# Keys and queries loaded in pieces twice as large in an attention and feed-forward kernel: 24 key loads of 768 KB in place of 48 of 384 KB, and the adds that pool them spread evenly

## The chip, the cores and the metric

One Trainium2 chip, one of its cores. The metric is the device time of one execution in microseconds (us). Three runs of the kernel before took 1876.52, 1888.96 and 1879.23 us; their median is 1879.23.

## The reference

Four batches of 12288 queries attend to 768 pooled keys, which are also the values; the result goes through a feed-forward block with a gated softmax and a layer norm. All in float32, with the feed-forward weights as float64:

```
kv_pool = kv.reshape(B, H//4, 4, W//4, 4, C).mean(axis=(2, 4))     # B=4, H=384, W=32, C=128
k = v = kv_pool.reshape(B, -1, C) @ w_sr                           # 768 keys
s = (q @ k.transpose(0, 2, 1)) / sqrt(C)                           # 12288 x 768 per batch
a = exp(s - max);  a /= a.sum + 1e-9;  x = a @ v
h = x @ w_in                                                       # 128 -> 1024
solu = h * softmax(h)
out = layernorm(solu) * g_ln @ w_out                               # 1024 -> 128
```

## The kernel before

**Tiles and slots.** The 49152 tokens are 384 tiles of 128; four tiles are a group (96 groups), 96 tiles a batch. The main loop runs over 384 slots. In slot s the scores and their exponential are those of tile s, and later stages work on earlier tiles: the hidden layer and its exponential on tile s - 10, its product u, the split of u into a high and a low half and their transpose on tile s - 11, the output matmuls on tile s - 13. All matmul operands are split in high and low halves, so most products are three matmuls. The order of instructions on every engine is the order in which the code is written (`manual_schedule`); each engine works through its own list in order.

**Engines.** TensorE (PE) does scores (L402), values (L456), hidden (L513) and output (L629). VectorE (DVE) does the row maxima (L419), the low half of the scores (phl, L430), the minimum over the hidden layer (L521), u (L554) and the reciprocals rz (L495). ScalarE (ACT) does the exponentials and squares. GpSimd (POOL) splits u (uhl: L578 high half, L585 low half), takes the low half of the queries once a group (ql, L390), prepares rz once a group (zz, L487, in slots that are 1 modulo 4, ahead of the split of u), computes the layer norm's root (f, L646 and L647, in slots that are 3 modulo 4), and adds up the keys (ka, L215). SyncE (SP) issues nearly all transfers, in one list: two DMA transposes per slot (pT, L433, of the scores, and uT, L589, of u), one load of queries and one store of results per group, and the key loads.

**Keys.** Each pooled key is a mean over 16 positions. Batch 0's keys are summed on TensorE at the start, out of 16 loads of two positions each for half the keys (`kv_first_load`, L163; `kv_first`, L176 and L179). For batches 1 to 3 each position is one load of 128 x 768 floats (`kv_load`, L204) into one of nine buffers (tag "kvc"), and POOL adds it to the sum in two halves (`kv_add`). `kv_plan` gives each load and add its slot: the load of a position in batch 2 or 3 stands at slots 3 modulo 4, two in twelve slots, and its adds three and five slots later, at the end of the slot. Batch 1 loads seven positions before the loop, with their adds placed by the table `SOON`, and the other nine from slot 7 on. `PLAN` then places the projection of the summed keys with w_sr, their norms and their split, in slots 60 to 95 of the batch before.

**Queries.** `q_load` (L373) loads one group, 128 x 512 floats, into one of three buffers, two groups ahead.

Of the kernel before, what the change touches and what calls it, by code (L numbers as in the profile page):

```python
# [11 lines left out]
F32 = mybir.dt.float32  # L12
F32R = mybir.dt.float32r
F16 = mybir.dt.float16
# [7 lines left out]
P = 128  # L22
B = 4
NTOK = 12288
NK = 768
RR = 16
DFF = 1024
# [27 lines left out]
IN_AT = 0  # L55
OUT_AT = 4

SOON = {0: (), 1: (-1, -1), 2: (8, 9), 3: (20, 22), 4: (24, 26), 5: (28, 30), 6: (32, 36)}
OUT0 = 6


# [1 line left out]
def kernel(  # L63
# [15 lines left out]
    nc = tc.nc  # L79

    dmt = ctx.enter_context(tc.tile_pool(name="dmt", bufs=2))
# [56 lines left out]
    state = {}  # L138
# [16 lines left out]
    def half_of(name, b, half):  # L155
        return state[name, b][:, half * 384 : half * 384 + 384]

    def kv_first_load(half, c):

        n = half * 8 + c  # L160
        tag, bufs = ("kvc", 9) if n < 9 else ("uT", 4) if n < 13 else ("uhl", 3)
        t = dmt.tile([P, 2, 384], F32, tag=tag, name=f"kv_{half}_{c}", bufs=bufs)
        nc.sync.dma_start(t, kv0[:, 2 * c : 2 * c + 2, half * 384 : half * 384 + 384])  # L163
        state["kv0", half, c] = t

# [31 lines left out]
        )  # L197
        nc.scalar.copy(half_of("kT", 0, half), pk)

    def kv_load(b, pos):  # L200

        t = dmt.tile([P, 2, 384], F32, tag="kvc", name=f"kv_{b}_{pos}", bufs=9)
        r, two = divmod(pos, 2)
        nc.sync.dma_start(  # L204
            t, kv[b - 1, r, :, two * NK : (two + 1) * NK].rearrange("p (h k) -> p h k", h=2)
        )
        state["kv", b, pos] = t

    def kv_add(b, half, pos):

# [108 lines left out]

    def kv_v_high(b, half):  # L320
        if half == 0:
            state["vhl", b] = dmt.tile([P, 2, NK], F16, tag="kvc", name=f"vhl_{b}", bufs=9)
        nc.gpsimd.tensor_scalar(
            state["vhl", b][:, 0, half * 384 : half * 384 + 384],
            half_of("ks", b, half),
            1.0,
            1.0,
            op0=ALU.mult,
            op1=ALU.mult,
        )  # L330
# [14 lines left out]
    def kv_plan(b):  # L345


        for pos in range(RR):


            if b == 1 and pos in SOON:
                for half, slot in enumerate(SOON[pos]):
                    yield slot, [partial(kv_add, b, half, pos)]
                continue

            n = pos - len(SOON) if b == 1 else pos
            slot = 12 * (n // 2) + 8 * (n % 2) + (7 if b == 1 else -37)
            yield slot, [partial(kv_load, b, pos)]
            if pos:
                yield slot + 3, [partial(kv_add, b, 0, pos)]  # L360
                yield slot + 5, [partial(kv_add, b, 1, pos)]
        for slot, part, *fs in PLAN:
            yield slot, [partial(f, b, part) for f in fs]


    QL = 1

    def q_load(g):
        if g >= NG or g % QL:
            return  # L370
        b, gb = divmod(g, GPB)
        t = dmt.tile([P, QL * 512], F32, tag="qf", name=f"qf_{g}", bufs=3)
        nc.sync.dma_start(t, qT[b, :, gb * 512 : (gb + QL) * 512])  # L373
        state["qf", g // QL] = t

    def q_split(g):
        if g >= NG:
            return
        qf = state["qf", g // QL][:, (g % QL) * 512 : (g % QL + 1) * 512]
        qh = grp.tile([P, 512], F32R, tag="qh", name=f"qh_{g}")  # L380
# [4 lines left out]
    def q_low(g):  # L385
        if g >= NG:
            return
        qf = state["qf", g // QL][:, (g % QL) * 512 : (g % QL + 1) * 512]
        qh, ql = state["q", g]
# [175 lines left out]
    def hidden_high(t):  # L565
        u, _ = state["u", t]
        if t in LOW_DVE:
            uhl = [
                dmt.tile([P, DFF], F16, tag="kvc", name=f"uhl_{t}_{a}", bufs=9) for a in range(2)
            ]  # L570
            state["uhl", t] = uhl
        else:
            state["uhl", t] = dmt.tile([P, 2, DFF], F16, tag="uhl", name=f"uhl_{t}", bufs=3)
            uhl = [state["uhl", t][:, a, :] for a in range(2)]
        if t in HIGH_ACT:
            nc.scalar.copy(uhl[0], u)  # L576
        else:
            nc.gpsimd.tensor_scalar(uhl[0], u, 1.0, 1.0, op0=ALU.mult, op1=ALU.mult)  # L578
        state["halves", t] = uhl
# [114 lines left out]
    for n in range(16):  # L694
        if n == IN_AT:
            nc.sync.dma_start(raw_in, w_in.bitcast(I32))
        if n == 4:
            q_load(0)
        if n == OUT_AT:
            nc.sync.dma_start(raw_out, w_out.bitcast(I32))  # L700
        kv_first_load(*divmod(n, 8))
    if OUT_AT == 16:
        nc.sync.dma_start(raw_out, w_out.bitcast(I32))
    q_load(1)
    for pos in SOON:
        kv_load(1, pos)
    nc.scalar.mul(w_sr16, wsr, 1.0 / RR)

    wf, wr, in_steps = float64_parts(raw_in, "in")
# [95 lines left out]
    def w_low():  # L805
# [4 lines left out]
        1: [w_sum, partial(kv_norm_max, 0, 0)],  # L810
        2: [partial(kv_scale_v, 0, 1), partial(kv_scale_v, 0, 2), partial(kv_now, 0, kv_vs),
            partial(kv_now, 0, kv_v_high), partial(kv_now, 0, kv_v_low)],
        3: [partial(kv_norm_max, 0, 1), w_scale],
        4: [partial(kv_v_turn, 0, 0), w_in_low],
# [19 lines left out]
        (84, 0, kv_bound), (87, 1, kv_bound), (88, 2, kv_bound),  # L834
        (89, 0, kv_vs), (90, 1, kv_vs),
        (91, 0, kv_v_high), (92, 0, kv_v_low), (93, 1, kv_v_high), (94, 1, kv_v_low),
        (95, 0, kv_v_turn),
    ]
# [20 lines left out]
    for b in range(1, B):  # L859
        for k, fs in kv_plan(b):  # L860
            plan.setdefault((b - 1) * TPB + k, []).append(fs)
# [4 lines left out]
    for slot in range(NT):  # L866
# [26 lines left out]
        at_soon(slot - NORM, values_norm)  # L893
        at_last(slot - FSC, final_scale)
        at(h0, hidden_high)
        at(h0, hidden_low)
        at_last(slot - FSC, final_root)
# [16 lines left out]
        if slot % GT == 0:  # L914
            q_load(slot // GT + 2)
# [11 lines left out]
    for i in range(NT - LH, NT + 1):  # L927
        k = i - (NT - LH)
        if k in (0, XH):
            g = G - 1 if k == 0 else G  # L930
# [17 lines left out]
        if i < LAST:  # L948
            hidden_high(i - 1)
            hidden_low(i - 1)  # L950
            if i < LAST - 1:
                hidden_var(i - 1)
        elif i == LAST:
            hidden_high(i - 1)
            hidden_turn_half(i - 1, 0)
# [60 lines left out]
```

## Time and profile before

| | |
|---|---|
| three runs | 1876.52, 1888.96, 1879.23 us |
| the profiled execution | 1880.71 us, of which 1878.9 from its first to its last instruction (the span) |
| TensorE clock granted | 0.998 |
| busy: PE, DVE, ACT, POOL | 98%, 95%, 93%, 87% of the span |
| key loads | 64 of 384 KB (16 of them batch 0's), 4.4 us from issue to landing (median) |
| query loads, stores of results | 96 of 256 KB, 3.4 us; 95 of 256 KB, 2.7 us |
| transposes uT, pT | 386 of 512 KB, 4.3 us; 384 of 384 KB, 4.0 us |

A row of a list of groups reads: line, engine, operation, output<-input, count; then busy time. A row in order of time reads: start in us, duration, engine, line, operation, and in brackets how long the engine stood before it and what ended that. SPq rows are the issue of a transfer, not the transfer. A row of a stretch gives its limits, its length, the busy time (and the number of instructions) of each engine that is named above it, the granted clock, the share of the DMA engines' time and GB/s.

### The profile page before, as it was taken

What the parts mean: (1) busy time and instruction counts of PE and PEld (TensorE: products, weight loads), DVE (VectorE), ACT (ScalarE), POOL (GpSimd) and SP (SyncE); (2) the same over time, 40 slices, a digit from 0 to 9 for tenths busy, and PEclk for the clock granted to TensorE, in tenths of its full rate; (3) what the DMA queues carried; (4) which work ended last, traced back from release to release, by engine and by line L of the source; (5) the groups of instructions that cost most, each with busy time, mean ns of one, the idle gap of its engine ahead of it and who ended that gap; (6) DMA issues with size and microseconds to landing.
All of it is one profiled execution on the core that took longest, in us unless ns stands there. A gap on an engine that the chain in (4) does not pass through costs nothing.

```text
span 1878.9 us, 43063 instructions
## 1 busy us (share of the span) xinstructions
PE 1837.0 (98%) x15676; PEld 1296.2 (69%) x15676; DVE 1787.7 (95%) x2692; ACT 1751.8 (93%) x3136; POOL 1630.9 (87%) x1400
## 2 busy tenths in 40 slices
PE   7899999999999999999999999999999999999997
PEld 5566777676676767767667767776677777777775
DVE  7899999999999999999999999999999999999996
ACT  4899999999999999999999999999999999999997
POOL 5899998999989888899988988888898888888886
PEclk9999999999999999999999999999999999999999
DMA  8999999999999999999999999999999999999998
GB/s 295 196 227 232 237 237 236 230 241 237 227 248 228 237 233 241 235 235 235 242 234 239 237 233 243 242 230 220 223 227 231 226 221 229 230 223 230 218 223 161
DMA packets 1483748, 434.43 MB, mean 231 GB/s; under 512 B 1411472, under 2 KB 1464848, under 8 KB 1483280
## 3 DMA queue, kind: packets, MB, share of 16 engines
q1 hardware_dynamic: 1483248, 431.60, 114.2%
q8 instruction: 124, 2.03, 0.5%
q14 instruction: 88, 0.72, 0.1%
q10 hardware_dynamic: 288, 0.07, 0.0%
HBM read 52.50 MB, written 25.17 MB: 41 GB/s over the span
## 4 chain that ended last, share of the span: by engine, by line
PE 66%; POOL 11%; DVE 10%; issue 6%; DMA 4%; ACT 3%; POOLq 0%; DVEq 0%; SPq 0%; ACTq 0%
PE o L629 19%; PE h L513 18%; PE s L402 15%; PE xa L456 14%; POOL uhl L585 4%; DMA uT<-uhl 3%; POOL uhl L578 3%; DVE junkd L521 2%; DVE nm L419 2%; DVE u L554 2%; DVE phl L430 2%; POOL ka L215 1%; DVE xl L472 1%; POOL ql L390 1%; ACT e L537 1%
## 5 line engine op out<-in xcount | busy, mean ns | idle before, releaser
L585 POOL TENSOR_TENSOR uhl<-u,uhl 128x1024 f16<-128x1024 f32 x382 | 815.7, 2136 | 33.5 <-ACT uhl L576 2.1
L629 PEld LDWEIGHTS <-uT 128*128 128x128 f16 x9216 | 545.0, 98 | 108.6 <-DMA uT<-uhl 22.5
L629 PE MATMUL o<-wch,uT 128*128 128x128 f16 x6144 | 577.2, 219 | 13.9 <-DMA uT<-uhl 12.8
L629 PE MATMUL o<-wcl,uT 128*128 128x128 f16 x3072 | 533.5, 219 | 0.0
L578 POOL TENSOR_SCALAR uhl<-u 128x1024 f16<-128x1024 f32 x377 | 394.8, 1047 | 150.8 <-DVE u L554 144.7
L554 DVE SCALAR_TENSOR_TENSOR u<-h,rz,e 128x1024 f32<-128x1024 f32 x384 | 491.3, 1279 | 29.3 <-ACT e L537 18.5
L521 DVE TENSOR_SCALAR_CACHE_REDUCE junkd<-h,rz 128x1024 bf16<-128x1024 f32 x384 | 491.1, 1279 | 4.6 <-PE h L513 4.1
L456 PE MATMUL xa<-pT,vT 128*128 128x512 f16 x1728 | 484.1, 381 | 1.7 <-DMA vT<-vhl 1.7
L537 ACT ACTIVATE e<-h,nm,rz 128x1024 f32<-128x1024 f32 x384 | 458.9, 1195 | 2.9 <-DVE junkd L521 2.9
L604 ACT ACTIVATE junk<-u,su 128x1024 bf16<-128x1024 f32 x384 | 438.1, 1141 | 0.2 <-DVE u L554 0.2
L419 DVE TENSOR_REDUCE nm<-s 128x1 f32<-128x768 f32 x384 | 364.9, 950 | 25.9 <-PE s L402 13.3
L420 ACT ACTIVATE s<-s,nm 128x768 f32<-128x768 f32 x384 | 335.4, 873 | 52.3 <-DVE nm L419 51.5
L430 DVE SCALAR_TENSOR_TENSOR phl<-s,phl 128x768 f16<-128x768 f32 x384 | 366.1, 953 | 2.5 <-ACT phl L422 2.5
L422 ACT ACTIVATE phl<-s 128x768 f16<-128x768 f32 x384 | 311.5, 811 | 14.1 <-DMA pT<-phl 2.0
L513 PEld LDWEIGHTS <-xh 128*128 128x128 f16 x1536 | 139.9, 98 | 198.3 <-DVE phl L430 31.7
L402 PE MATMUL s<-kh,qh 128*128 128x384 f32 x768 | 256.3, 415 | 9.4 <-DVE u L554 3.9
L456 PEld LDWEIGHTS <-vT 128*128 128x128 f16 x1728 | 139.5, 98 | 141.6 <-issue 57.1
L513 PE MATMUL h<-w_in_h,xh 128*128 128x512 f16 x768 | 228.7, 379 | 5.8 <-DVE phl L430 3.2
L513 PE MATMUL h<-w_in_h,xl 128*128 128x512 f16 x768 | 228.4, 379 | 0.0
L513 PE MATMUL h<-w_in_l,xh 128*128 128x512 f16 x768 | 228.4, 379 | 0.0
L402 PE MATMUL s<-kh,ql 128*128 128x384 f32 x768 | 197.0, 338 | 0.0
L402 PE MATMUL s<-kl,qh 128*128 128x384 f32 x768 | 195.1, 335 | 0.0
(121 smaller groups left out, 1686.2 us busy)
## 6 DMA issues: line engine op xcount, KB each, us to landing
kv<-in_kv_dram SPq DMA_DIRECT2D x64, 384.0 KB, 4.4
qf<-in_q_dram SPq DMA_DIRECT2D x96, 256.0 KB, 3.4
out_dram<-ob SPq DMA_DIRECT2D x95, 256.0 KB, 2.7
uT<-uhl SPq DMA_TRANSPOSE x386, 4.3
pT<-phl SPq DMA_TRANSPOSE x384, 4.0
raw_in<-in_moe_w_in_dram SPq DMA_DIRECT2D x1, 1024.0 KB, 5.2
raw_out<-in_moe_w_out_dram SPq DMA_DIRECT2D x1, 1024.0 KB, 8.0
out_dram<-ob SPq DMA_DIRECT2D x2, 128.0 KB, 1.8
```

What stands on the lines that cost most here:

```text
L402: nc.tensor.matmul(s[:, half, :384], lh[:, ts], rh[:, half * 384 : (half + 1) * 384], start=n == 0, stop=n == 2,)
L419: nc.vector.tensor_reduce(nm, s, axis=AX.XY, op=ALU.max, negate=True)
L430: nc.vector.scalar_tensor_tensor(phl[:, 1], state.pop(("s", t)), SC, phl[:, 0], op0=ALU.mult, op1=ALU.subtract)
L456: nc.tensor.matmul(xa, vT[:, v * NKC + c, :], pT[:, :, a * NKC + c, :], start=n == 0, stop=n == len(seq) - 1,)
L513: nc.tensor.matmul(h[:, hs], lh[:, ts], rh[:, hs], start=n == 0, stop=n == 2)
L521: nc.vector.tensor_scalar(junk, state["h", t], state["rz", g][1][:, j : j + 1], None, op0=ALU.mult, op1=ALU.min, accum_out=nm,)
L537: nc.scalar.activation(e, state["h", t], AF.Exp, bias=nm, scale=state["rz", g][0][:, js], accum_out=state["z2", g][:, js],)
L554: nc.vector.scalar_tensor_tensor(u, state.pop(("h", t)), state["rz", g][2][:, j : j + 1], state.pop(("e", t)), op0=ALU.mult, op1=ALU.mult, ...
L578: nc.gpsimd.tensor_scalar(uhl[0], u, 1.0, 1.0, op0=ALU.mult, op1=ALU.mult)
L585: engine.tensor_tensor(low, u, high, op=ALU.subtract)
L604: nc.scalar.activation(junk, u, AF.Square, scale=-float(DFF), bias=su, accum_out=state["v3", g][:, j : j + 1],)
L629: nc.tensor.matmul(po[:, ts], uT[:, a * NFC + c, :], w[:, c, :], start=start, stop=stop)
```

## The change

Three things. `QL` becomes 2: one query load brings two groups (512 KB), in two buffers instead of three. `kv_load` brings two positions at once (768 KB, 6144 bytes in a row per partition) into one of five buffers of two; in batches 2 and 3 one such load stands in every twelve slots, at slots 2 modulo 4, and its four adds 2, 5, 8 and 11 slots later. For batch 1 four such loads (eight positions) stand before the loop, the other four at slots 6, 18, 30 and 42, and 28 adds at an even pace from slot 9 to 57 in place of the table. Batch 0's loads stay as they are; ten of them (before nine) share the key buffers, now two by two. The line numbers of the changed kernel are 5 to 7 higher.

```diff
-SOON = {0: (), 1: (-1, -1), 2: (8, 9), 3: (20, 22), 4: (24, 26), 5: (28, 30), 6: (32, 36)}
+SOON = 4
@@ kv_first_load
-        tag, bufs = ("kvc", 9) if n < 9 else ("uT", 4) if n < 13 else ("uhl", 3)
-        t = dmt.tile([P, 2, 384], F32, tag=tag, name=f"kv_{half}_{c}", bufs=bufs)
+        if n < 10:
+            if n % 2 == 0:
+                state["kv0", n] = dmt.tile(
+                    [P, 2, 2, 384], F32, tag="kvc", name=f"kv_{half}_{c}", bufs=5
+                )
+            t = state["kv0", n - n % 2][:, n % 2]
+        else:
+            tag, bufs = ("uT", 4) if n < 14 else ("uhl", 3)
+            t = dmt.tile([P, 2, 384], F32, tag=tag, name=f"kv_{half}_{c}", bufs=bufs)
...
-    def kv_load(b, pos):
-        t = dmt.tile([P, 2, 384], F32, tag="kvc", name=f"kv_{b}_{pos}", bufs=9)
-        r, two = divmod(pos, 2)
-        nc.sync.dma_start(
-            t, kv[b - 1, r, :, two * NK : (two + 1) * NK].rearrange("p (h k) -> p h k", h=2)
-        )
-        state["kv", b, pos] = t
+    def kv_load(b, r):
+        t = dmt.tile([P, 2, 2, 384], F32, tag="kvc", name=f"kv_{b}_{r}", bufs=5)
+        nc.sync.dma_start(t, kv[b - 1, r].rearrange("p (w h k) -> p w h k", w=2, h=2))
+        for w in range(2):
+            state["kv", b, 2 * r + w] = t[:, w]
@@ kv_plan
-        for pos in range(RR):
-            if b == 1 and pos in SOON:
-                for half, slot in enumerate(SOON[pos]):
-                    yield slot, [partial(kv_add, b, half, pos)]
-                continue
-            n = pos - len(SOON) if b == 1 else pos
-            slot = 12 * (n // 2) + 8 * (n % 2) + (7 if b == 1 else -37)
-            yield slot, [partial(kv_load, b, pos)]
-            if pos:
-                yield slot + 3, [partial(kv_add, b, 0, pos)]
-                yield slot + 5, [partial(kv_add, b, 1, pos)]
+        for r in range(RR // 2):
+            slot = 12 * r - 42
+            if b > 1 or r >= SOON:
+                yield slot, [partial(kv_load, b, r)]
+            for n in range(4):
+                pos, half = 2 * r + n // 2, n % 2
+                if not pos:
+                    continue
+                if b > 1:
+                    at = slot + 3 * n + 2
+                elif pos == 1:
+                    at = -1
+                else:
+                    at = 9 + 9 * (4 * (r - 1) + n) // 5
+                yield at, [partial(kv_add, b, half, pos)]
...
-    QL = 1
+    QL = 2
...
-        t = dmt.tile([P, QL * 512], F32, tag="qf", name=f"qf_{g}", bufs=3)
+        t = dmt.tile([P, QL * 512], F32, tag="qf", name=f"qf_{g}", bufs=2)
...
-    for pos in SOON:
-        kv_load(1, pos)
+    for r in range(SOON):
+        kv_load(1, r)
```

First place: POOL in slots 22 to 25, before. A name is the tile, its own number (the batch and position of keys, the tile of uhl, the group of zz and ql) and a running number.

```order
L390 TENSOR_TENSOR ql_6_1335<-qf_6_958,qh_6_1334 128x512
L215 TENSOR_TENSOR ka_1_261<-ka_1_261,kv_1_3_161 128x384
L215 TENSOR_TENSOR ka_1_261<-ka_1_261,kv_1_9_1181 128x384
L578 TENSOR_SCALAR uhl_12_1424<-u_12_1410 128x1024
L585 TENSOR_TENSOR uhl_12_1424<-u_12_1410,uhl_12_1424 128x1024
L646 TENSOR_TENSOR f_2_1421<-f2_2_1422,v3_2_1003 128x4
L647 TENSOR_TENSOR f2_2_1422<-f_2_1421,mhalf_85 128x4
L578 TENSOR_SCALAR uhl_13_1492<-u_13_1481 128x1024
L585 TENSOR_TENSOR uhl_13_1492<-u_13_1481,uhl_13_1492 128x1024
L215 TENSOR_TENSOR ka_1_261<-ka_1_261,kv_1_4_163 128x384
L215 TENSOR_TENSOR ka_1_261<-ka_1_261,kv_1_9_1181 128x384
L487 TENSOR_SCALAR zz_4_1564<-z_4_916,bb_0_116 128x4 x2
```

The same place in the change, where kv_1_3 holds positions 6 and 7:

```order
L397 TENSOR_TENSOR ql_6_1315<-qf_6_939,qh_6_1314 128x512
L585 TENSOR_SCALAR uhl_12_1402<-u_12_1388 128x1024
L592 TENSOR_TENSOR uhl_12_1402<-u_12_1388,uhl_12_1402 128x1024
L653 TENSOR_TENSOR f_2_1399<-f2_2_1400,v3_2_985 128x4
L654 TENSOR_TENSOR f2_2_1400<-f_2_1399,mhalf_85 128x4
L220 TENSOR_TENSOR ka_1_248<-ka_1_248,kv_1_3_154 128x384
L585 TENSOR_SCALAR uhl_13_1471<-u_13_1460 128x1024
L592 TENSOR_TENSOR uhl_13_1471<-u_13_1460,uhl_13_1471 128x1024
L494 TENSOR_SCALAR zz_4_1541<-z_4_897,bb_0_116 128x4 x2
```

Of four adds between ql of group 6 and zz of group 4 one is left, and none stands directly before zz.

Second place: SP in slots 102 to 105, before (phl_102 is slot 102's).

```order
L433 DMA_TRANSPOSE pT_25_7084<-phl_102_7210 128x12x128
L589 DMA_TRANSPOSE uT_91_7271<-uhl_91_7223 128x16x128
L433 DMA_TRANSPOSE pT_25_7084<-phl_103_7276 128x12x128
L589 DMA_TRANSPOSE uT_92_7341<-uhl_92_7292 128x16x128
L204 DMA kv_2_7_7343<-in_kv_dram 128x768
L433 DMA_TRANSPOSE pT_26_7375<-phl_104_7349 128x12x128
L589 DMA_TRANSPOSE uT_93_7409<-uhl_93_7362 128x16x128
L373 DMA qf_28_7411<-in_q_dram 128x512
L433 DMA_TRANSPOSE pT_26_7375<-phl_105_7419 128x12x128
```

The same place in the change:

```order
L440 DMA_TRANSPOSE pT_25_7033<-phl_102_7157 128x12x128
L596 DMA_TRANSPOSE uT_91_7218<-uhl_91_7170 128x16x128
L210 DMA kv_2_4_7220<-in_kv_dram 128x1536
L440 DMA_TRANSPOSE pT_25_7033<-phl_103_7225 128x12x128
L596 DMA_TRANSPOSE uT_92_7290<-uhl_92_7241 128x16x128
L440 DMA_TRANSPOSE pT_26_7322<-phl_104_7296 128x12x128
L596 DMA_TRANSPOSE uT_93_7356<-uhl_93_7309 128x16x128
L380 DMA qf_28_7358<-in_q_dram 128x1024
L440 DMA_TRANSPOSE pT_26_7322<-phl_105_7367 128x12x128
```

The key load stands one slot earlier and brings two positions; the query load stays and brings two groups.

Third place: POOL in slots 103 to 105, with the add of the keys just named. Before:

```order
L578 TENSOR_SCALAR uhl_93_7362<-u_93_7351 128x1024
L585 TENSOR_TENSOR uhl_93_7362<-u_93_7351,uhl_93_7362 128x1024
L487 TENSOR_SCALAR zz_24_7432<-z_24_6764,bb_1_647 128x4 x2
L578 TENSOR_SCALAR uhl_94_7436<-u_94_7421 128x1024
L585 TENSOR_TENSOR uhl_94_7436<-u_94_7421,uhl_94_7436 128x1024
L578 TENSOR_SCALAR uhl_95_7513<-u_95_7502 128x1024
L585 TENSOR_TENSOR uhl_95_7513<-u_95_7502,uhl_95_7513 128x1024
L390 TENSOR_TENSOR ql_27_7495<-qf_27_7120,qh_27_7494 128x512
L215 TENSOR_TENSOR ka_2_4910<-ka_2_4910,kv_2_7_7343 128x384
```

In the change:

```order
L585 TENSOR_SCALAR uhl_93_7309<-u_93_7298 128x1024
L592 TENSOR_TENSOR uhl_93_7309<-u_93_7298,uhl_93_7309 128x1024
L220 TENSOR_TENSOR ka_2_4284<-ka_2_4284,kv_2_4_7220 128x384
L494 TENSOR_SCALAR zz_24_7380<-z_24_6714,bb_1_631 128x4 x2
L585 TENSOR_SCALAR uhl_94_7384<-u_94_7369 128x1024
L592 TENSOR_TENSOR uhl_94_7384<-u_94_7369,uhl_94_7384 128x1024
```

The first add of the new keys moves from the end of slot 106, behind ql, to the end of slot 104, directly before zz.

More of the change, by code (lines that the diff above doesn't have):

```diff
@@ L321, in kv_v_high @@
         if half == 0:
-            state["vhl", b] = dmt.tile([P, 2, NK], F16, tag="kvc", name=f"vhl_{b}", bufs=9)
+            state["vhl", b] = dmt.tile([P, 2, NK], F16, tag="kvc", name=f"vhl_{b}", bufs=5)
         nc.gpsimd.tensor_scalar(
@@ L568, in hidden_high @@
             uhl = [
-                dmt.tile([P, DFF], F16, tag="kvc", name=f"uhl_{t}_{a}", bufs=9) for a in range(2)
+                dmt.tile([P, DFF], F16, tag="kvc", name=f"uhl_{t}_{a}", bufs=5) for a in range(2)
             ]
```

## The prediction

> **What bounds the kernel now.** A slot is one token tile's pass through the loop, 384 in all. I read the busy shares first, then cut the span at slot starts and counted the row maxima (L419, one per slot) in each stretch.
>
> ```profile
> PE 1837.0 (98%) x15676; PEld 1296.2 (69%) x15676; DVE 1787.7 (95%) x2692; ACT 1751.8 (93%) x3136; POOL 1630.9 (87%) x1400
> core 0: us, DVE busy (x), PEclk, DMA share, GB/s
> 124.10:202.00 77.90, 15.20 (x16) 1.00 1.14 230
> 202.00:468.30 266.30, 53.21 (x56) 1.00 1.19 236
> 468.30:926.20 457.90, 91.29 (x96) 1.00 1.19 236
> 926.20:1228.80 302.60, 60.89 (x64) 1.00 1.20 237
> 1228.80:1380.80 152.00, 30.37 (x32) 1.00 1.14 225
> 1380.80:1792.20 411.40, 83.64 (x88) 1.00 1.14 227
> ```
>
> The last row is the measure: no keys are loaded or added there, and 88 slots take 411.40, so 4.675 us a slot, TensorE busy without a break. That pace does not depend on anything the diff touches. Against it the earlier stretches (slots 24, 40, 96, 192, 256 on) lose: 77.90 - 16 x 4.675 = **3.1** us, 4.5, 9.1, 3.4 and 2.4. The 2.4 (slots 256 to 287) holds neither a key load nor a key add, only the projection and scaling of the next keys (PLAN). That work also falls into the stretches from 40 and from 96, and stays. So what loads and adds can cost is 3.1 in the first stretch and 4.5 + 9.1 + 3.4 - 2 x 2.4 = **12.2** later: 15.3 us, 0.8% of the kernel, is the most that steady running can give back. The ramp before slot 24 has its adds moved by a slot or two and the tail keeps its work; I count nothing for either.
>
> Who makes TensorE late? The waits from 100 to 1792 us:
>
> ```profile
> PEld L629 <- DMA uT<-uhl: 14.2, 20, 1.8
> PE o L629 <- DMA uT<-uhl: 5.7, 10, 1.4
> DVE rz L495 <- POOL zz L487: 4.3, 5, 1.4
> ```
>
> Two things: transposed hidden tiles that land late (14.2 at the weight loads, near the 12.2 above), and zz, which VectorE awaits for rz.
>
> **First loss: POOL's adds.** Slots 22 to 25 on POOL, then VectorE in slot 25 (start, duration), and the busy times of all engines in the stretch without adds (PE, PEld, DVE, ACT, POOL):
>
> ```profile
> 122.82 1.97 POOL L215 TENSOR_TENSOR ka<-ka,kv 128x384 f32<-128x384 f32 x2
> 124.76 1.05 POOL L578 TENSOR_SCALAR uhl<-u 128x1024 f16<-128x1024 f32 x1
> 125.89 2.14 POOL L585 TENSOR_TENSOR uhl<-u,uhl 128x1024 f16<-128x1024 f32 x1
> ...
> 132.49 1.98 POOL L215 TENSOR_TENSOR ka<-ka,kv 128x384 f32<-128x384 f32 x2
> 134.56 0.62 POOL L487 TENSOR_SCALAR zz<-z,bb 128x4 f32<-128x4 f32 x2
> 131.04 0.08 DVE L554 DVE_READ_ACCUMULATOR u<-h,rz,e 128x1 f32 x1
> 132.91 0.95 DVE L430 SCALAR_TENSOR_TENSOR phl<-s,phl 128x768 f16<-128x768 f32 x1
> 135.21 0.20 DVE L495 RECIPROCAL rz<-zz 128x8 f32<-128x8 f32 x1 [1.35 <-POOL zz L487]
> 1380.80:1792.20 411.40, 411.40 (x3566) 293.01 (x3566) 400.88 (x595) 395.10 (x706) 344.69 (x288) 1.00 1.14 227
> ```
>
> Without adds (last row, POOL's 344.69 in 88 slots) POOL works 15.7 us in four slots of 18.7: room 3.0, three adds of 0.98. The old table puts 15 adds into slots 20 to 36, 3.5 per four slots or 3.5 us, and two of them directly before zz in slots 25 and 33; VectorE then stands 1.35 us. The new list gives 28 adds in slots 9 to 57, 2.3 per four slots or 2.2 us, and never two in one slot. From slot 20 to 24 six adds become two, so POOL reaches the zz of slot 25 well over the 1.35 earlier. I take the whole **-3.1** (bounds -3.1 and 0). What is late next there is TensorE itself. In batches 2 and 3 the pairs two slots apart become one add every three slots, 1.3 per four slots as before; I count nothing for it.
>
> **Second loss: the one DMA queue.** SP's rows (start, time to issue) from slot 102's hidden tile to slot 104's query load; two rows of a stretch without keys; the seven early key loads of the start with the query load behind them; and, from 193.8 to 1229 us, how many loads of which size there are and how long they take to land:
>
> ```profile
> 508.56 2.02 SPq L589 DMA_TRANSPOSE uT<-uhl  x1
> 510.67 1.51 SPq L433 DMA_TRANSPOSE pT<-phl  x1
> 512.29 1.82 SPq L589 DMA_TRANSPOSE uT<-uhl  x1
> 514.16 0.57 SPq L204 DMA_DIRECT2D kv<-in_kv_dram  x1
> 514.83 1.41 SPq L433 DMA_TRANSPOSE pT<-phl  x1
> 516.34 3.48 SPq L589 DMA_TRANSPOSE uT<-uhl  x1
> 519.86 0.57 SPq L373 DMA_DIRECT2D qf<-in_q_dram  x1
> 1421.30 1.80 SPq L589 DMA_TRANSPOSE uT<-uhl  x1
> 1423.78 1.39 SPq L433 DMA_TRANSPOSE pT<-phl  x1
> 19.00 6.27 SPq L204 DMA_DIRECT2D kv<-in_kv_dram  x7
> 25.50 0.33 SPq L373 DMA_DIRECT2D qf<-in_q_dram  x1
> kv<-in_kv_dram SPq DMA_DIRECT2D x36, 384.0 KB, 4.2
> qf<-in_q_dram SPq DMA_DIRECT2D x54, 256.0 KB, 3.4
> ```
>
> With keys each issue starts as the one before ends; without them SP rests (1423.10 to 1423.78). A transpose behind a load takes 3.48 instead of 1.82: the queue is full, and a hidden tile that falls behind costs TensorE. The bytes stay. From slot 40 to 256 the 54 query loads become 27 and the 36 key loads (these counts are of 193.8 to 1229 us) become 18: 45 transfers fewer. What does one cost besides its bytes? A pair of transposes takes 514.16 - 510.67 = 3.5 us. Twenty-four slots of 4.77 us (the stretch from 468.30) hold 24 pairs and 16 plain transfers (4 of keys, 6 of queries, 6 of results), so these have (114.5 - 84) / 16 = 1.9 us each. At the start, where seven loads go out in 6.5 us, 384 KB is 0.93, and 288 KB, the mean of the sixteen, 0.7. So a removed transfer gives back between 0 (all is bytes, slowed by the transposes beside them) and 1.2 us. I take 0.45, nearer to the bytes, since the startup loads follow each other with nothing in between: 45 x 0.45 = 20 us of 1030, 2% of the queue. Against it stand the larger parcels: 768 KB at once hold the next transpose 0.9 to 1.9 us longer than 384 do. Of the 12.2 I take half, **-6.1** (bounds -12.2, and +12 if each of the 20 waits doubles).
>
> The Trainium skill, "DMA: Bandwidth & Descriptors", section on the anatomy of one DMA, fits a transfer as about 2.0 us fixed plus its bytes at 436 GB/s (measured on the path issued from GpSimd). By it, an estimate, 45 transfers fewer would free 90 us of the queue, and every late tile of this kind would go. The row of seven loads at 0.93 us each speaks against adding that fixed part where transfers overlap.
>
> **Third: a wait that the change adds.** For batches 2 and 3 the first half of a load's first position is now added two slots after the load, before it was three; and the load is twice as large. Both happen at fixed places: load at a slot 2 mod 4, add at the end of a slot 0 mod 4, and directly behind it on POOL zz of the next slot. Behind that add wait zz, both hidden steps of a tile, and for zz VectorE. There are 14 such places (seven loads in two batches; the first load of a batch is first read eight slots later; batch 1 loads at least ten slots ahead). Before, the add read keys that had long landed: the load of 514.16 landed near 518.4 and was read at 523.85.
>
> ```profile
> 523.85 1.00 POOL L215 TENSOR_TENSOR ka<-ka,kv 128x384 f32<-128x384 f32 x1
> 513.70 0.08 DVE L554 DVE_READ_ACCUMULATOR u<-h,rz,e 128x1 f32 x1
> 512.40 0.62 POOL L487 TENSOR_SCALAR zz<-z,bb 128x4 f32<-128x4 f32 x2
> 392.02 1.76 SPq L589 DMA_TRANSPOSE uT<-uhl  x1
> 399.40 0.08 DVE L554 DVE_READ_ACCUMULATOR u<-h,rz,e 128x1 f32 x1
> ```
>
> VectorE wants zz 2.75 us after u of its slot (133.86 after 131.12 above). Slot 102: the new load goes out after the transpose that ends at 510.6, and lands 4.2 + 0.9 to 1.9 later, at 515.7 to 516.7; add 1.0 and zz 0.6 end at 517.3 to 518.3; VectorE wants zz at 513.8 + 2.75 = 516.5. Loss 0.8 to 1.8. Slot 78: out at 393.8, zz by 400.5 to 401.5, wanted at 399.5 + 2.75 = 402.2. No loss. So the 14 places cost between 0 and 25 us as the queue stands. With the queue some 1 us shorter, as the term before has it, slot 102 is left with 0 to 0.8 and slot 78 with nothing; between the two I take 0.24 a place: 14 x 0.24 = **+3.3**.
>
> **The start.** The first query load is 512 KB and stands ahead of twelve of the first keys' loads. At 0.93 per 384 KB these land 0.6 later. POOL waits for them:
>
> ```profile
> 22.93 2.96 POOL L176 TENSOR_TENSOR kv<-kv 128x384 f32<-128x384 f32 x2 [1.12 <-DMA kv<-in_kv_dram]
> 29.36 0.45 PE L402 MATMUL s<-kh,qh 128*128 128x384 f32 x1 [1.05 <-ACT kh L189]
> ```
>
> and behind POOL TensorE's projection and the first scores: **+0.6** (bounds 0 and 0.7). The eighth early position goes out behind these and is first read at slot 23; the second query load, now part of the first, was not waited for. Nothing for both. Queries are split five slots or more after their load, as before: nothing.
>
> **Sum.** The profiled execution took 1880.7 (span 1878.9, 1.8 around it), 1.5 above the median of the three, 1879.2. 1880.7 + 0.6 - 3.1 - 6.1 + 3.3 = 1875.4; half of the 1.5 taken off for the median, **1874.5**.
>
> **Rivals.** (a) Every queue wait goes, and the adds never wait: 1880.7 + 0.6 - 3.1 - 12.2 = 1866. For it: the queue needs only to fall below the 4.675 pace for a while to drain, as it does without keys. Against: the parcels. The floor of TensorE's 4.675 ends it there. The Trainium skill's fixed part per transfer, on the page named above, leads to this case. (b) The queue goes by bytes alone: nothing off the 12.2, and the adds wait 0.3 at each place: 1880.7 + 0.6 - 3.1 + 4 = 1882. For it: the seven loads' even spacing. (c) Slower: the add on 768 KB just issued blocks POOL. If loads land 1 us later than worked out above, slot 102 loses 1.8 to 2.8 and slot 78 up to 0.3, 1.2 a place between them; 14 x 1.2 = 17, while the uT waits shrink by some 3 because TensorE stands elsewhere: 1880.7 + 0.6 - 3.1 - 3 + 17 = 1892. It decides from a landing 1.6 us (add and zz) before zz is wanted: at slot 102 that is 514.9, already passed; at slot 78 it is 400.6, with 0.7 to 1.7 us to spare. Against it: a waiting POOL gives the queue time, which brings the next load forward.
>
> **Chances.** Forecast (1870 to 1879) 0.5; (a) 0.17; (b) 0.2; (c) 0.13. Range 1864 to 1888: it takes in (a) and (b) and leaves out most of (c). About 1% is what a measurement of this kernel can tell from no change, 18.8 us; 15.3 is the most that can be given back, so faster than that 0.02, slower 0.05, within it 0.93.
>
> **What the changed profile would show.** Slots 24 to 39 at 75 us and no wait of rz for zz before 202 us (first term). In 202 to 1229 us SP pauses again, and uT waits of about 7 instead of 14 (second). POOL's add waiting for the key load at slots 68, 80, 92, 104 and on, and rz for zz behind it (third, and (c)). First scores at 30.0 instead of 29.4 (start). Wrong I would be above all if the 14 adds find their keys late, or if the pace without keys were not 4.675 any more.

## The result, and the profile after

The changed kernel takes 1904.1 us (median of four runs, 1897.1 to 1907.0) beside 1881.1 for the kernel before in the same session: **ratio 1.0112, 95% interval 1.0091 to 1.0133**, so 21 us slower, where 1874.5 was predicted and 1864 to 1888 given as the range. Ratios, here and below, compare fast executions alone, so they can differ a little from those of the medians, and one execution of run 7, which took 6731 us with TensorE busy for 6716 of them, is not in its ratio. The profiled execution of the changed kernel took 1907.0; its span is 1905.2, 26.3 us more than that of before. The page's first part, and the same cut at slot starts as in the prediction (slots 24, 40, 96, 192, 256, 288, 376; row maxima, now L426):

```profile
PE 1841.1 (97%) x15676; PEld 1299.3 (68%) x15676; DVE 1789.6 (94%) x2692; ACT 1752.2 (92%) x3136; POOL 1627.9 (85%) x1400
core 0: us, DVE busy (x), PEclk, DMA share, GB/s
125.04:201.54 76.50, 15.23 (x16) 1.00 1.21 234
201.54:475.91 274.37, 53.28 (x56) 0.99 1.18 230
475.91:944.15 468.24, 91.44 (x96) 1.00 1.19 231
944.15:1255.38 311.23, 60.90 (x64) 0.99 1.20 230
1255.38:1406.99 151.61, 30.42 (x32) 1.00 1.16 223
1406.99:1819.04 412.05, 83.66 (x88) 1.00 1.15 226
```

Busy times hardly differ: the work is the same, the waits are not. The pace without keys is as before (412.05 for 88 slots, 411.40 before). Slots 24 to 39 gain 1.4 us (77.90 before), and all loss lies where keys are loaded: 274.37 for 56 slots (266.30), 468.24 for 96 (457.90), 311.23 for 64 (302.60). That is 27 us. The main waits for transfers from 100 to 1810 us, and VectorE's for zz (total us, times, longest):

```profile
POOL ka L220 <- DMA kv<-in_kv_dram: 27.0, 11, 4.6
PEld L636 <- DMA uT<-uhl: 22.4, 23, 2.1
PE xa L463 <- DMA pT<-phl: 17.3, 11, 2.7
PE o L636 <- DMA uT<-uhl: 11.7, 15, 1.6
DVE rz L502 <- POOL zz L494: 10.8, 7, 2.0
PEld L463 <- DMA pT<-phl: 6.4, 5, 2.5
```

The waits for uT went from 14.2 + 5.7 to 22.4 + 11.7. Two waits are new. POOL waits for keys (the prediction's third term) and rz for zz behind it, 10.8 instead of 4.3. And TensorE waits 23.7 us for **pT**, the transposed probabilities of the values matmuls, which the prediction did not look at. Waits of matmuls and of weight loads overlap in such a list, so here is the time from slot 40 to 256 in which TensorE did neither, added up from the trace: 29.4 us, where it was 8.1 before. Ahead of the values matmuls it is 19.0 more (none before), mostly for pT; ahead of the output matmuls, for uT, 4.2 more (10.1 after 5.9); elsewhere 1.9 less. One place shows it, slots 136 to 139: rows of SP's list, then POOL, VectorE and TensorE.

```profile
680.11 0.57 SPq L380 DMA_DIRECT2D qf<-in_q_dram  x1
...
688.53 3.06 SPq L596 DMA_TRANSPOSE uT<-uhl  x1
691.65 0.57 SPq L210 DMA_DIRECT2D kv<-in_kv_dram  x1
692.31 1.40 SPq L440 DMA_TRANSPOSE pT<-phl  x1
...
697.41 0.99 POOL L220 TENSOR_TENSOR ka<-ka,kv 128x384 f32<-128x384 f32 x1 [3.10 <-DMA kv<-in_kv_dram]
698.49 0.61 POOL L494 TENSOR_SCALAR zz<-z,bb 128x4 f32<-128x4 f32 x2
699.14 0.20 DVE L502 RECIPROCAL rz<-zz 128x8 f32<-128x8 f32 x1 [1.24 <-POOL zz L494]
699.17 1.02 PE L463 MATMUL xa<-pT,vT 128*128 128x512 f16 x4 [1.81 <-DMA pT<-phl]
```

The 768 KB of keys land at 697.3, 5.7 us after the start of their issue. POOL has waited 3.10 for them, zz comes 1.24 late. Directly behind the load on the queue stands pT of tile 139, the fourth of its group. It lands at 698.9, and TensorE has waited 1.81. Before, the load stood behind that transpose, not ahead of it. In the chain of work that ended last the DMA's share is 9%, where it was 4% before:

```profile
PE 63%; DVE 10%; DMA 9%; issue 6%; ACT 6%; POOL 5%; DVEq 0%; POOLq 0%; SPq 0%; ACTq 0%
```

### The profile page after: what moved, and what is told of

It reads as the page before. It is cut to its first block, busy times and chain, and to the rows that moved or that the text cites. A ratio compares the mean times of both kernels' runs of the same rounds, so it can differ in the third digit from the quotient of the medians.

```text
span 1905.2 us, 42994 instructions
## 1 busy us (share of the span) xinstructions
PE 1841.1 (97%) x15676; PEld 1299.3 (68%) x15676; DVE 1789.6 (94%) x2692; ACT 1752.2 (92%) x3136; POOL 1627.9 (85%) x1400
## 4 chain that ended last, share of the span: by engine, by line
PE 63%; DVE 10%; DMA 9%; issue 6%; ACT 6%; POOL 5%; DVEq 0%; POOLq 0%; SPq 0%; ACTq 0%
PE o L636 18%; PE h L520 17%; PE s L409 14%; PE xa L463 13%; DMA uT<-uhl 5%; DMA pT<-phl 3%; DVE nm L426 2%; DVE junkd L528 2%; POOL uhl L592 2%; DVE u L561 2%; DVE phl L437 2%; ACT e L544 2%; POOL uhl L585 2%; ACT junk L611 2%; ACT phl L429 1%
## 5 line engine op out<-in xcount | busy, mean ns | idle before, releaser
L426 DVE TENSOR_REDUCE nm<-s 128x1 f32<-128x768 f32 x384 | 365.3, 951 | 44.4 <-PE s L409 34.5
```

Of the source, the lines that this page charges most:

```text
L426: nc.vector.tensor_reduce(nm, s, axis=AX.XY, op=ALU.max, negate=True)
```

## The experiments

Every run was timed in several rounds beside the kernel before on the same chip; ratios are to that kernel. The main theories: **P**, the key load's place ahead of pT; **A**, the adds that wait for keys; **B**, a burst of bytes at one place; and, from the later runs of 7 on, **S**, the size of a single transfer. The expectations name the others where they need them.

| run | ratio, 95% interval | median us |
|---|---|---|
| changed kernel | 1.0112 (1.0091 to 1.0133) | 1904.1 |
| 1. adds later | 1.0098 (1.0080 to 1.0116) | 1900.5 |
| 2. load behind pT, adds later | 1.0047 (1.0031 to 1.0063) | 1890.2 |
| 3. single query loads | 1.0017 (1.0005 to 1.0029) | 1884.0 |
| 4. kernel before, key loads a slot earlier | 0.9994 (0.9983 to 1.0006) | 1880.8 |
| 5. kernel before, query pairs | 1.0022 (1.0009 to 1.0035) | 1886.6 |
| 6. 1 to 3 together | 0.9969 (0.9957 to 0.9980) | 1876.5 |
| 7. key loads halved, and once more | 1.0014 (1.0001 to 1.0027), 1.0025 (1.0001 to 1.0049) | 1885.3, 1884.4 |
| 8. kernel before, even adds | 0.9982 (0.9970 to 0.9993) | 1879.3 |
| 9. query loads halved | 1.0020 (1.0010 to 1.0031) | 1884.5 |
| 10. both halved | 0.9961 (0.9946 to 0.9975) | 1875.2 |
| 11. run 6 with keys halved | **0.9942** (0.9927 to 0.9957) | 1871.2 |
| 12. gaps of 32 bytes | 1.1008 (1.0988 to 1.1027) | 2070.4 |
| 13. halved by partitions | 1.0116 (1.0096 to 1.0135) | 1901.5 |
| 14. run 11 with loads halved again | 1.0025 (1.0011 to 1.0039) | 1884.6 |
| 15. gaps of 512 bytes, queries only | 1.0083 (1.0067 to 1.0099) | 1896.5 |
| 16. kernel before, buffers shifted | 1.1014 (1.0996 to 1.1031) | 2072.1 |

**1. Adds later.**

```diff
-                    at = slot + 3 * n + 2
+                    at = slot + 3 * n + 5
```

> The changed kernel with the eight key adds of each position pair of batches 2 and 3 three slots later (first add five slots behind its load instead of two); loads, queries and batch 1 as changed. Theory P (place: the key load stands on SP's queue directly ahead of the transpose pT of a tile 3 mod 4, which TensorE's values matmuls need two slots later): TensorE still waits about 20 us for pT, only POOL's 27 us of waits for keys go, with some 5 to 8 us of waits for zz behind them: 1896 to 1900. Theory A (adds: POOL waits for keys just loaded, zz and rz wait behind it, all else follows): POOL waits for no key, and the kernel is back at 1880 to 1886.

```profile
PE xa L463 <- DMA pT<-phl: 11.0, 7, 2.6
PEld L463 <- DMA pT<-phl: 4.1, 4, 2.1
```

All 27.0 us of POOL's waits for keys and the zz waits behind them are gone, and the kernel gained some 3 us, which the intervals don't separate from nothing. TensorE still waits 15.1 for pT. Theory A falls as the main cause.

**2. Load behind pT, adds later.**

```diff
-            slot = 12 * r - 42
+            slot = 12 * r - 41
-                    at = slot + 3 * n + 2
+                    at = slot + 3 * n + 4
```

> The changed kernel with its key loads one slot later (3 mod 4, so issued right behind pT of that tile instead of ahead of it) and the adds of batches 2 and 3 three slots later than in the changed kernel, as in the run with the adds alone later. Theory P: TensorE's wait for pT falls from 24 us to under 6, and the kernel to 1876 to 1884, 13 us or more below the run with the adds alone later. Theory A: the same as that run, within 3 us. Theory Z (parcel size: 768 KB and 512 KB hold up whatever is queued behind them): no gain over that run either, the waits move from pT to uT.

```profile
PEld L636 <- DMA uT<-uhl: 33.2, 33, 3.0
PE o L636 <- DMA uT<-uhl: 19.3, 19, 2.5
```

The place is worth 10 us over run 1, and no wait for pT is left; but 52.5 us of waits for uT (34.1 in the changed kernel) show that the queue is still behind. The time in which TensorE does nothing, slots 40 to 256, falls from 25.5 us in run 1 to 18.2, and now 17.7 of it stand ahead of the output matmuls. P has a part, not the whole.

**3. Single query loads.**

```diff
-    QL = 2
+    QL = 1
-        t = dmt.tile([P, QL * 512], F32, tag="qf", name=f"qf_{g}", bufs=2)
+        t = dmt.tile([P, QL * 512], F32, tag="qf", name=f"qf_{g}", bufs=3)
```

> The changed kernel with queries loaded for one group at a time again (256 KB, three buffers); keys as changed. Theory Z (size of the parcels, the 512 KB of queries in the slot before the key load above all): the pT waits behind loads at slots 2 mod 8 shrink by half, and the kernel falls by 8 to 14 us to 1890 to 1896. Theory P: the place of the key load is what costs, pT waits at every load as before, 1898 to 1904. If each transfer cost a fixed 0.45 us beside its bytes, as predicted, 27 more of them would add up to 12 us.

More than any theory expected: 18 us come back, with 27 transfers more in the stretch with keys.

**4. The kernel before with its key loads a slot earlier.**

```diff
-            yield slot, [partial(kv_load, b, pos)]
+            yield slot - 1, [partial(kv_load, b, pos)]
```

> The kernel before with nothing changed but its key loads (384 KB) one slot earlier, at slots 2 mod 4, ahead of pT of the tile 3 mod 4 instead of behind it; adds where they were. Theory P: pT waits appear in a kernel that had none, 4 to 10 us of them at half the size of parcel, and the kernel takes 1884 to 1891. Theories A and Z: no difference, within 3 us of the kernel before, since the adds wait for nothing (four slots behind their load) and no parcel has grown.

```profile
PEld L629 <- DMA uT<-uhl: 6.4, 12, 0.8
PE xa L456 <- DMA pT<-phl: 5.5, 6, 1.8
```

The pT waits appear as P says, 5.5 us, and the time stays: the uT waits fell from 14.2 to 6.4 at the same time. The place ahead of pT costs nothing with 384 KB. It costs with large loads (run 2).

**5. The kernel before with query pairs**: `QL = 2`, two buffers.

> The kernel before with only the queries loaded for two groups at once (512 KB, two buffers). Theory Q (the query pair alone is what costs, since the changed kernel with single query loads was 20 us faster): 1895 to 1902. Theory B (burst: each big load uses up part of the 1 to 2.5 us that the transposed tiles have to spare, and only a 512 KB query load with a 768 KB key load two slots behind it uses up more than that): 1881 to 1887, with uT waits somewhat above the 20 us of before and no pT waits. The prediction's fixed 0.45 us per transfer: 27 transfers fewer are worth 12 us of the queue, 1877 or less.

4 us slower than before: not Q's 1895 to 1902, and nothing of the 12 us that a fixed part per transfer would have saved. It is B's range.

**6. Single queries, load behind pT, adds later**: the edits of runs 1 to 3 together.

> The changed kernel with all three remedies: single query loads, key loads one slot later (behind pT of the tile 3 mod 4) and the adds of batches 2 and 3 three slots later. What is left of the change is the 768 KB key loads and the even adds of batch 1. Theory B: no pT waits, no waits for keys, uT waits as before, and the 3 us of zz waits before slot 40 gone: 1875 to 1880. Theory N (a 768 KB parcel by itself costs, wherever it stands): 1882 to 1886, with uT waits above 25 us.

1876.5, faster than before by 0.3%. Only the keys are still large.

**7. Key loads halved, at the same place.**

```diff
-        nc.sync.dma_start(t, kv[b - 1, r].rearrange("p (w h k) -> p w h k", w=2, h=2))
+        for w in range(2):
+            nc.sync.dma_start(
+                t[:, w],
+                kv[b - 1, r, :, w * NK : (w + 1) * NK].rearrange("p (h k) -> p h k", h=2),
+            )
```

> The changed kernel with each 768 KB key load issued as two loads of 384 KB, one behind the other, into the halves of the same buffer, at the same slots. If a transfer costs something beside its bytes (0.45 us as predicted), the kernel gets slower by some 5 to 10 us: 1909 to 1914. If the queue goes by bytes and what costs is the burst at one place: the same as the changed kernel within 3 us, 1901 to 1907. If single large transfers are what blocks, and 384 KB ones let transposes through: below 1897.

> The kernel with halved key loads (two of 384 KB at the place of each 768 KB) once more, since the profiled execution of the first such run fell on a chip whose TensorE ran at a quarter of its speed, so that its waits say nothing; its times gave 1885 against 1904 of the changed kernel. Theory S (a single transfer of 768 KB takes the queue longer than two of 384 KB, or lets less through beside it): 1882 to 1888, and from the landing ahead of a key load to its own some 3.3 us (twice 1.65) instead of 3.6 to 3.8; pT and key waits mostly gone. Theory B (burst of bytes) expects the changed kernel's time, 1901 to 1907.

The waits of the second run:

```profile
PEld L640 <- DMA uT<-uhl: 17.0, 20, 1.8
PE xa L467 <- DMA pT<-phl: 6.5, 5, 2.3
POOL ka L224 <- DMA kv<-in_kv_dram: 3.2, 2, 2.3
```

The same bytes at the same slots, in more transfers, and 16 to 18 us faster. Theory B falls for the keys, and so does the saving per transfer.

**8. The kernel before with even adds.**

```diff
-                for half, slot in enumerate(SOON[pos]):
+                for half in range(2 if pos else 0):
+                    slot = -1 if pos == 1 else 9 + 9 * (2 * pos - 4 + half) // 5
...
-                yield slot + 3, [partial(kv_add, b, 0, pos)]
-                yield slot + 5, [partial(kv_add, b, 1, pos)]
+                even = b == 1 and pos < 12
+                for half in range(2):
+                    at = 9 + 9 * (2 * pos - 4 + half) // 5 if even else slot + 3 + 2 * half
+                    yield at, [partial(kv_add, b, half, pos)]
```

> The kernel before with only the adds of batch 1 (positions 2 to 11) spread as in the change, one every two slots or so from slot 9 on; all loads as before. The prediction's first term (POOL's burst of adds holds up zz in slots 24 to 40): 3 us faster, 1877 to 1879, and no wait of rz for zz before 202 us. If something else is late there next (the queue): 1880 to 1882, same as before.

The stretch of slots 24 to 39 (row maxima):

```profile
124.16:198.96 74.80, 15.21 (x16) 1.00 1.21 237
```

16 times 4.675 is 74.80: the whole 3.1 us of that stretch is gone, and the ratio gives 3.4 us.

**9. Query loads halved, and 10. both halved.** Keys as in run 7; queries:

```diff
-        nc.sync.dma_start(t, qT[b, :, gb * 512 : (gb + QL) * 512])
+        for w in range(QL):
+            ws = slice(w * 512, w * 512 + 512)
+            nc.sync.dma_start(t[:, ws], qT[b, :, (gb + w) * 512 : (gb + w + 1) * 512])
```

> The changed kernel with each 512 KB query load issued as two of 256 KB, one behind the other, at the same slots; key loads 768 KB as changed. Theory S for queries as for keys: 1882 to 1890, like the run with single query loads. Theory B: the bytes stand at the same place, so no change, 1901 to 1907; then what the single query loads gained came from spreading them.

> The changed kernel with both kinds of load halved, keys and queries, at the same slots: bytes and places of the change, number and size of transfers of the kernel before. Theory S: the size was all, 1876 to 1883. Theory B: 1901 to 1907. A mixture: 1884 to 1892.

Both halved, cut at the same slots from 40 to 256, and the waits that are left:

```profile
199.00:466.49 267.49, 53.33 (x56) 1.00 1.19 236
466.49:920.89 454.40, 91.42 (x96) 1.00 1.18 238
920.89:1222.88 301.99, 60.90 (x64) 1.00 1.18 237
PEld L642 <- DMA uT<-uhl: 5.4, 9, 1.7
PE o L642 <- DMA uT<-uhl: 2.0, 2, 1.2
POOL ka L224 <- DMA kv<-in_kv_dram: 1.2, 2, 0.9
PE xa L469 <- DMA pT<-phl: 0.5, 1, 0.5
```

This is the run that settles the sign (TensorE stands idle for 7.2 us in slots 40 to 256, for 29.4 in the change). Bytes, places, buffers and adds are those of the change; only its merging is undone, and the ratio falls from 1.0112 to 0.9961, **28 us**. Every wait of the change shrinks to a trifle, those of POOL for keys too (27.0 to 1.2), though the adds stand where the change put them. Spreading the queries again (run 3) gains nothing over halving them in place (run 9): what costs is the large transfer, not the burst.

Where the queue spends it is seen in the landings in the traces between 202 and 1229 us: from the landing of the transpose ahead of a load to that of the transpose behind it, mean over the loads (17 of keys and 27 of queries with the merged slots; single ones spread by some 0.6 to 1.2 us).

| | before | changed | keys halved | queries halved | both halved |
|---|---|---|---|---|---|
| key load with its transpose | 3.5 (384 KB) | 5.8 (768 KB) | 5.0 | 5.3 | 5.1 |
| query load with its transpose | 3.0 (256 KB) | 4.9 (512 KB) | 4.8 | 4.1 | 4.4 |
| a transpose behind a transpose | 2.0 | 2.0 | 2.0 | 2.0 | 2.0 |

In the changed kernel a merged key load takes the queue 0.7 to 0.8 us longer than its two halves at the same place take in the two other kernels; beside halved queries it takes only 0.2 longer (5.3 and 5.1). For a merged query load it is 0.5 to 0.8 throughout. Twenty-four slots hold two of the one and three of the other: 2 x 0.7 + 3 x 0.5 = 2.9 us. Between the changed kernel and both halved lie (468.24 - 454.40) / 4 = 3.5 us in 24 slots. So the longer intervals make up most of the loss between these two kernels. They do not make up the 11 us that halving the keys still gave once the queries were halved (run 9 to run 10): there 17 x 0.2 is 3.4 us, and the query loads were no shorter. That the longer transfers are the whole way in which merging costs is therefore not shown; that merging costs is.

The two parts don't add up: undoing either gives 16 to 18 us, undoing the second then 10 to 12 more. In the run that puts the load behind pT the merged loads took 5.4 and 4.5 at the same sizes, less than the 5.8 and 4.9 of the changed kernel, though with this spread that is barely a difference.

**11. Run 6 with its key loads halved.**

> The run with all three remedies (single queries, keys one slot later, adds three later: 1876.5) with each key load also halved into two of 384 KB. Theory S: 768 KB costs there too, 1872 to 1875. Theory B or a bound elsewhere (uT waits): the same within 2 us, 1875 to 1879.

```profile
PEld L640 <- DMA uT<-uhl: 7.8, 11, 1.4
PE o L640 <- DMA uT<-uhl: 3.4, 6, 0.9
```

The fastest version tried, 0.58% faster than the kernel before (its interval overlaps that of run 10): query loads of 256 KB, key loads of 384 KB, two at one place behind pT, with adds that start four slots behind them and batch 1's adds even.

**12. Short rows by gaps of 32 bytes.** Is it the length of a row (6 and 4 KB a partition) or the transfer as such?

```diff
-        t = dmt.tile([P, 2, 2, 384], F32, tag="kvc", name=f"kv_{b}_{r}", bufs=5)
+        t = dmt.tile([P, 2, NK + 8], F32, tag="kvc", name=f"kv_{b}_{r}", bufs=5)
...
-        t = dmt.tile([P, QL * 512], F32, tag="qf", name=f"qf_{g}", bufs=2)
+        t = dmt.tile([P, QL, 520], F32, tag="qf", name=f"qf_{g}", bufs=2)
```

> The changed kernel with single transfers of 768 and 512 KB, but into buffers with 32 bytes left free between their halves, so that each partition is written in two rows of 3 KB (keys) or 2 KB (queries) instead of one of 6 or 4 KB. If the length of a row is what costs: 1873 to 1880, like the run with both kinds halved (1875). If the transfer as such costs: 1901 to 1907.

It missed by over 160 us, for a reason that run 16 sorts out. The loads themselves took 5.0 (keys) and 4.3 (queries) with their transpose, like halved ones, but in a kernel that ran 10% slower, so this tells little.

**13. Long rows, two transfers of 64 partitions.**

```diff
+        for n in range(2):
+            ps = slice(64 * n, 64 * n + 64)
+            nc.sync.dma_start(t[ps], qT[b, ps, gb * 512 : (gb + QL) * 512])
```

(and the keys in the same way)

> The changed kernel with each 768 KB and each 512 KB load issued as two, each for 64 partitions, at the same slots: transfers of 384 and 256 KB, but rows of 6 and 4 KB as changed. If the length of a row costs: 1901 to 1907. If the transfer as such costs: 1873 to 1880.

```profile
qf<-in_q_dram SPq DMA_DIRECT2D x54, 256.0 KB, 4.2
kv<-in_kv_dram SPq DMA_DIRECT2D x34, 384.0 KB, 5.5
```

No gain: in these long rows two transfers cost what one costs. From issue to landing they take 4.2 and 5.5 us in the median, where halves of the same sizes in short rows, issued at the same places, take 3.6 (run 9) and 4.6 (run 7):

```profile
qf<-in_q_dram SPq DMA_DIRECT2D x54, 256.0 KB, 3.6
kv<-in_kv_dram SPq DMA_DIRECT2D x34, 384.0 KB, 4.6
```

Rows are twice as long there and partitions half as many; this run doesn't part the two.

**14. Run 11 with its loads halved again**: keys in four of 192 KB (rows of 1.5 KB), queries in two of 128 KB (rows of 1 KB).

> The best run so far (single queries, keys in halves one slot later, adds three later: 1871.2) with each of its loads cut in two again: keys as four of 192 KB in rows of 1.5 KB, queries as two of 128 KB in rows of 1 KB. If shorter rows or smaller transfers go on gaining as from the change to its halves: 1863 to 1868 (the floor by the pace without keys is about 1862 to 1865). If each further transfer costs a fixed part by now: 1873 to 1885. If neither: 1869 to 1873.

```profile
PEld L641 <- DMA uT<-uhl: 30.8, 31, 2.3
PE o L641 <- DMA uT<-uhl: 16.7, 18, 1.8
```

16 us lost against run 11, and 1884.6 is within what was expected if each further transfer costs a fixed part by now. In the landings a key load in four with its transpose takes 5.2 us (5.0 in two, run 11), a query load in two 3.4 (3.0 in one). Rows became shorter as well, so a fixed part per transfer and the shorter rows aren't told apart. The gain from smaller pieces has an end; of the sizes tried, rows of 2 and 3 KB in transfers of 256 and 384 KB are best.

**15. Gaps of 512 bytes, for the queries alone**: buffers of `[P, QL, 640]`, one transfer, two rows of 2 KB.

> The changed kernel with each 512 KB query load still one transfer, but into a buffer with 512 bytes left free between its halves, so that a partition is written in two rows of 2 KB instead of one of 4 KB; every DMA buffer stays at a multiple of 512 bytes. If the length of a row is what costs: 1882 to 1888, like the run with the query loads halved (1884.5), and query load plus the next transpose take some 4.2 us of the queue instead of 4.9. If the transfer as such costs: 1900 to 1907.

Between both expectations: 5.5 us of the 17 that halving the query loads gave. A load with its transpose took 4.75 (4.9 changed, 4.1 halved). So shorter rows in one transfer bring about a third (the two intervals only just keep it from nothing), and two transfers with long rows bring nothing; of what was tried, only both together, halves by columns, bring all of it. What inside the transfer makes up the rest stays open.

**16. The kernel before with all DMA buffers 64 bytes further on.**

```diff
-    dmt.tile([P, 96], F32, tag="pad", name="pad", bufs=1)
+    dmt.tile([P, 112], F32, tag="pad", name="pad", bufs=1)
```

> The kernel before with every DMA buffer 64 bytes further on (the pad tile ahead of them 448 bytes instead of 384), so none at a multiple of 512 any more; nothing else changed. If the place of the buffers is what made the run with short rows slow: 2040 to 2080, with a pace without keys of about 5.1 us a slot instead of 4.675. If it was the split rows: 1878 to 1885.

The last 88 slots, without keys:

```profile
1524.38:1973.79 449.41, 84.01 (x88) 1.00 1.14 207
```

5.11 us a slot instead of 4.675, with no row shortened. Run 12 has the same pace there, 451.02 us for 88 slots or 5.125, and its gaps also move the buffers behind them by multiples of 64 bytes; run 15, whose gaps keep multiples of 512 bytes, has 411.82. So the place of the buffers is enough for run 12's miss.

## Why the prediction was wrong, step by step

**Second loss, the failed step.** It gave each removed transfer 0.45 us, taken from the gap between 0.7 us a load at the start and 1.9 us in the loop, and -6.1 in sum. The merging measured +28 (run 10), outside the bound of +12 too. The gap was not time that a merged transfer saves: no row of before showed a larger transfer in the loop, and there the larger one takes mostly 0.5 to 0.8 us more than its halves. The size was of that order; the sign was wrong. Rival (a), which took all 12.2 back, falls with it. The Trainium skill's fixed 2.0 us per transfer ("DMA: Bandwidth & Descriptors", anatomy of one DMA), by which, an estimate, 45 fewer would have freed 90 us, finds no support where the merged loads were halved, and neither does the rule of the section on bandwidth in the same page to batch transfers to 1 MiB and more: here two of 384 KB beat one of 768 KB (run 7, 16 to 18 us). Below 384 and 256 KB more transfers did cost time (run 14), by 0.2 and 0.4 us for each load that was split, in shorter rows.

**What was left out.** The prediction's "768 KB at once hold the next transpose 0.9 to 1.9 us longer than 384 do" was priced for uT alone (the bound of +12); pT had no term. The transpose directly behind a key load at a slot 2 modulo 4 is pT of its group's last tile, wanted two slots later. Before, it landed mostly 1 to 2.5 us ahead of TensorE in the stretches with keys, and the larger load takes 1.9 to 2.3 more than a load of before (5.8 and 4.9 against 3.5 and 3.0). The order rows in the change showed the new neighbour; who waits for it was not asked. By the time in which TensorE stood idle most of the loss shows at this place; run 2 puts its worth at some 10 us, since behind pT the large load is late for uT instead, and run 4 shows that it is free at the old size.

**Third, the adds.** The mechanism came as described, at the places named, and POOL waited 27.0 us, just above the 25 that the working gave as the most. Keys landed 6.0 us after their issue, at the upper end of the 5.1 to 6.1 that were worked out:

```profile
kv<-in_kv_dram SPq DMA_DIRECT2D x17, 768.0 KB, 6.0
```

Yet taking all of it away gave 3 us (run 1), about the term's +3.3. That is luck: the term priced a place at 0.24 us, where 11 places held POOL for 2.5 each. The rows of slots 136 to 139 show why so little came of it: where POOL waited, TensorE was waiting for pT as well. Rival (c) was thus right on its wait and wrong that this would set the time.

**First loss.** Right: run 8 gives 3.4 us, and no wait of rz for zz is left in the stretch. In the changed kernel only 1.4 of it show; with the queries halved the same stretch takes 74.9, so the large query loads took the rest.

**Rival (b)** was right that nothing is saved per transfer, and wrong that bytes alone count.

**The start.** +0.6 did not show: the first scores begin at 29.32 (29.36 before).

```profile
29.32 0.44 PE L409 MATMUL s<-kh,qh 128*128 128x384 f32 x1 [0.52 <-ACT kh L196]
```

**The pace without keys** held, as the whole argument needed.

**Left over.** With the merging undone the change is 7 us faster than before (0.9961), of which the even adds explain 3.4; for the rest, run 4 (0.9994) and the queries' earlier second half are candidates that the intervals don't separate.

## What to carry to other kernels

On a queue that transposes share and fill, a larger transfer wasn't cheaper here for being one: try its halves at the same place before counting a saving, and the next smaller size too, since the gain ended there. For each transfer that moves, name the one directly behind it in the queue, who waits for that, and how many us it has to spare. Taking away the largest wait in a list gives little where another engine is late at the same place.

## What the runs showed of the hardware that was not expected

- Shape of a transfer: 384 KB in 64 rows of 6 KB took 5.5 us to land, in 128 rows of 3 KB 4.6 (runs 13 and 7; row length and number of partitions not told apart). Rows of 1.5 and 1 KB in twice as many transfers lost 16 us against 3 and 2 KB (run 14).
- Placement: 64 bytes of shift of every DMA buffer in on-chip memory made the kernel before 10.1% slower, and every slot without keys 0.43 us longer. By their sizes in the code the buffers had all lain at one offset from the multiples of 512 bytes, multiples themselves by the run's expectation; no trace shows an address. The Trainium skill ("DMA: Bandwidth & Descriptors", how a descriptor splits into AXI transactions) has a transaction that reads start at a multiple of 256 bytes, which points the same way; that this is the mechanism was not shown.
- A large load's cost may not be fixed: 512 KB with its transpose took 4.9 us in the changed kernel and 4.5 with the key load one slot later, each a mean of 27 with a spread of 0.9 to 1.0.
